# Attention by clusters, then a gated layer: shifts first in a period, a division in another order, an earlier opening

## The chip, the cores and the metric

The kernel runs on one core of a Trainium2 chip. A core has a matrix engine (TensorE, PE in the profile), a vector engine (VectorE, DVE), an engine for curves and copies (ScalarE, ACT), a general one (GpSimd, POOL) and one that here only issues transfers (SyncE, SP). They work beside each other and wait for each other through semaphores; each takes its own instructions in order. SBUF is the memory on the chip and PSUM the small one, in eight banks, that matmuls write. The metric is the device time of one execution in microseconds (us).

## The reference

Two stages. The first is attention in which a query sees only the keys that chose the same one of 16 centroids; the second is a layer with the activation h * erf(softplus(h)).

```python
batch, n_heads, seq, head_dim = (4, 8, 768, 64)
q_assign = np.argmax(np.einsum('bhsd,hcd->bhsc', q_n, c_n), axis=-1)
k_assign = np.argmax(np.einsum('bhsd,hcd->bhsc', k_n, c_n), axis=-1)
mask = q_assign[:, :, :, None] == k_assign[:, :, None, :]
scores = scale * np.matmul(q, k.transpose(0, 1, 3, 2))
scores = np.where(mask, scores, -1000000000.0)
scores = scores - np.max(scores, axis=-1, keepdims=True)
attn = np.exp(scores)
attn = attn / (np.sum(attn, axis=-1, keepdims=True) + 1e-09)
return np.matmul(attn, v).astype(np.float32)
...
h = x @ w_in                      # x: 3072 x 512, w_in: 512 x 2048
sp = np.maximum(h, 0.0) + np.log1p(np.exp(-np.abs(h)))
g = h * erf(sp)
return (g @ w_out).astype(np.float32)
```

`q_n`, `k_n` and `c_n` are q, k and the centroids divided by their lengths.

## The kernel before

**Pairs, halves, units, periods.** Two heads are worked on together as a pair, in the two halves of the 128 partitions; there are 16 pairs. The queries of a pair come in two halves of 384, the keys in six blocks of 128, so a pair has 12 units (`units`), each a block of scores of 128 keys by 2 x 384 queries. `period(p, i)` handles two units; six periods (i = 0 to 5) make a pair, the first three its half 0, the last three its half 1.

**Score and shift.** `products` writes q times k into a bank pair `sc` (two such buffers). `scores` adds, by a second matmul of the 0/1 masks `qm` and `km`, a large negative number where the clusters differ, and for each query a shift, so that the exponential on ACT (`curve`, into one of eight buffers `pr`) needs no maximum of its own. The shift must be known first: `maxima_step` recomputes the masked scores in bf16 with queries on the partitions into the bank pair `wide` (a matmul of `qv` and `kv`, then one of `qm` and `km`), and DVE takes their maximum (`nmx`). A pair needs 12 such steps. After six of them a small reduction makes `lowest`, and `turn` transposes it with three matmuls into a bank `turned[h]`, from which ACT copies one row for each head into `qm`: the row of shifts. `scores` of that half can start only then.

**How far ahead.** A list `ahead` (L689) says which maxima steps belong to which unit: mostly the step seven further on, with one step of pair 1 left out and done by itself at the end of pair 0. `turn` stands before the scores in periods 2 and 5 (L732), one period before the shift is used.

**Sums and division.** `accumulate` adds up the exponentials on POOL, `attend` multiplies them with v into `turned[half]`, both for the units of the period before. When a half is complete (at the end of periods 3 and 0 of the next pair), `divide` sums over partitions with a matmul of -1s (`minus`) into the other `turned` bank and makes 1/sum as exp(-ln(sum)) on ACT (`inv`). In the next period DVE makes one Newton step on it (`den`, two operations) and then the quotient `x`, which reads `turned[half]`; SP stores it in DRAM.

**Choosing.** For the pair after next, `transposes` turns q and k on DVE, `similarities` multiplies by the centroids into `turned[1]`, `choose` finds the winner, and `masks` multiplies by `pick` into a `turned` bank and copies to `qm` or `km` on ACT. `MASKS` (L47) says in which period and at which of four places of it: 0 after the first maxima step, 1 after the products, 2 between the two exponentials, 3 at the end. So the two `turned` banks serve the output, the sums, the similarities, the masks and the shifts in turn.

**Weights.** In spare time, ACT, DVE and POOL convert the layer's weights, which come as 64-bit floats (`size_and_rest`, `bounded`, `sign`, `shifted`, `summed`): two pieces of 512 columns in a pair, 22 pieces in the first 11 pairs. From about 465 us only the layer runs.

**The order.** In the attention all instructions keep the order in which the program writes them on each engine (`InOrder`), so the code above is the schedule. DMAs wait for their slot, for the buffer they write and for the engine that read it last. The opening (L174 to L200, L249 to L279, L794 to L849) loads the centroids and pair 0's q and k from two queues, normalizes the centroids, makes constants, transposes, chooses and does the first seven maxima steps of pair 0.

Of the kernel before, what the change touches and what calls it, by code (L numbers as in the profile page):

```python
# [9 lines left out]
F32 = mybir.dt.float32  # L10
# [9 lines left out]
P = 128  # L20
B, H, S, D = 4, 8, 768, 64
C = 16
# [21 lines left out]
NPT = NJ + 2  # L44
N_LATE = 10
LAST_X = 11
MASKS = {(0, 1): ("k", 0), (0, 2): ("k", 1), (2, 0): ("q", 0), (5, 0): ("q", 1)}  # L47
FIRST_MASKS = {(2, 1): ("k", 0), (2, 3): ("q", 0), (3, 0): ("k", 1), (5, 0): ("q", 1)}


class InOrder:
# [16 lines left out]
def kernel(  # L68
# [65 lines left out]
    def part_of(i, lo, n):  # L134
        return more_out[:, i].rearrange("p f m -> p (f m)")[:, lo : lo + n]
# [14 lines left out]
    def load(p, nm, src, pl):  # L150
        if p >= NPAIR:
            return
        b, h0 = heads(p)
        if nm == "v":
            t = pl.tile([P, NJ, 2, D], F32, name="in_v")
            for e in range(2):
                queues[0].dma_start(out=t[:, :, e], in_=src[b, h0 + e].rearrange("(j p) d -> p j d", p=P))
        else:

            t = pl.tile([P, NB, Q], F32, name="in_" + nm)  # L160
            for e in range(2):
                for g in range(D // Q):
                    queues[e].dma_start(
                        out=t[e * D + g * Q : e * D + (g + 1) * Q],
                        in_=src[b, h0 + e, :, g * Q : (g + 1) * Q].rearrange("(n t) d -> t n d", t=Q),
                    )
        pairs.setdefault(p, {})[nm] = t

    def load_qk(p):
        load(p, "q", q, stage)  # L170
        load(p, "k", k, stage)


    setup = prs[-1].rearrange("p e n -> p (e n)")  # L174
# [2 lines left out]

    load_qk(0)
    queues[1] = sy
    tc.keep_in_program_order(nc.scalar.preload_act_table_set("natural_log_exp_and_others"))  # L180

    make_identity(nc, ident)
# [60 lines left out]
    def summed(n):  # L243
        w, lo = w_steps[n][0].bitcast(I32), steps[n][1].bitcast(I32)
        ge.tensor_tensor(out=w, in0=w, in1=lo, op=ALU.add)
        if n in after_of:
            fetch(after_of[n])

    cn = setup[:, D : 3 * D].rearrange("p (e d) -> p e d", e=2)  # L249
    spare = iter(range(3 * D, HW))  # L250

    def scalar_tile():
        n = next(spare)
        return setup[:, n : n + 1]
# [6 lines left out]
    norm = scalar_tile()  # L261
    ae.activation(out=norm, in_=ss, func=ACT.Ln)
    ae.activation(out=norm, in_=norm, func=ACT.Exp, scale=0.5)
    for it in range(2):
        inv = scalar_tile()
        ve.reciprocal(out=inv, in_=norm)
        twice = scalar_tile()
        ve.scalar_tensor_tensor(
            out=twice, in0=ss, scalar=inv, in1=norm, op0=ALU.mult, op1=ALU.add
        )  # L270
        norm = scalar_tile()
        ve.tensor_scalar(
            out=norm, in0=twice, scalar1=0.5, scalar2=(1e-6 if it else 0.0),
            op0=ALU.mult, op1=ALU.add,
        )
    rden = scalar_tile()
    ve.reciprocal(out=rden, in_=norm)
    for e in range(2):
# [2 lines left out]
    def transposes(p, which="qk"):  # L281

        if p >= NPAIR:
            return
        st = pairs[p]
        for nm in which:
            st[nm + "T"] = rows[p % 3][nm]
            ve.transpose(out=st[nm + "T"], in_=st.pop(nm).rearrange("p n t -> p (n t)"))
        if "k" in which:
            st.update(lows[p % 2])  # L290
            load_qk(p + 1)

    def similarities(p):

# [77 lines left out]
    def turn(p, h):  # L372

        st = pairs[p]
        pn = turned[h][:, 0:HW].rearrange("p (t n) -> p t n", t=HJ)
        for t in range(HJ):
            te.matmul(pn[:, t], lhsT=lowest[h][:, t], rhs=identb, start=True, stop=True)
        for e in range(2):
            r = slice(e * D + SH, e * D + SH + 1)
            ae.copy(  # L380
                out=st["qm"][r, h * HW : (h + 1) * HW], in_=pn[r].rearrange("p t n -> p (t n)")
            )
        st["shift", h] = True
# [34 lines left out]
    def curve(u):  # L418

        pr = prs[u % NPT]  # L420
        ae.activation(out=pr[:, :, 0:HW], in_=sc_of.pop(u)[:, :, 0:HW], func=ACT.Exp, scale=D**-0.5)
# [25 lines left out]
    def divide(u):  # L447

        p, half, _ = units[u]
        st = pairs[p]  # L450
        av = st["av", half]

        psum = turned[1 - half][:, 0:HW]
        for e in range(2):
            te.matmul(
                psum[e * D : (e + 1) * D], lhsT=minus, rhs=st["acc", half][:, e], start=True, stop=True
            )

        if u + 1 < len(units):
            inv = routep.tile([P, HW], F32, name="inv")  # L460
            den = routep.tile([P, HW], F32, name="den")
        else:
            inv, den = part_of(0, 4 * HW, HW), part_of(1, 0, HW)
        ae.activation(out=inv, in_=psum, func=ACT.Ln, bias=alleps, scale=-1.0)
        ae.activation(out=inv, in_=inv, func=ACT.Exp, scale=-1.0)
        yield
        ve.scalar_tensor_tensor(
            out=den, in0=psum, scalar=S * EPS, in1=inv, op0=ALU.subtract, op1=ALU.mult
        )
        ve.scalar_tensor_tensor(  # L470
            out=den, in0=den, scalar=2.0, in1=inv, op0=ALU.add, op1=ALU.mult
        )
        yield
        x = part_of(0, (2 * p + half) % 4 * HW, HW)
        ve.scalar_tensor_tensor(
            out=x, in0=av[:, 0:HW], scalar=av[:, HW : HW + 1], in1=den, op0=ALU.add, op1=ALU.mult
        )
        b, r = divmod(p, HP)
        nc.sync.dma_start(
            out=x_dram[r * P : (r + 1) * P, b * S + half * HW : b * S + (half + 1) * HW], in_=x  # L480
        )
        if half == 1:
            del pairs[p]
        yield
# [201 lines left out]

    ahead = [[] for _ in units]  # L689
    for n in range(NJ + 1, 2 * NJ * NPAIR):  # L690
        if n == 3 * NJ:
            continue
        slot = n - NJ - (n < 2 * NJ or n > 3 * NJ)
        if slot < len(units):
            ahead[slot].append(divmod(n, 2 * NJ))

    def step_ahead(slot):
        for which in ahead[slot]:
            maxima_step(*which)

    forms = sum((left_forms(ve, *w_in_parts(f, 2)) for f in range(0, HF, 2)), [])
    routing = [iter(())]
# [2 lines left out]
    def period(p, i):  # L705
# [7 lines left out]
                return masks(p + 1, *which, turned[0 if i in (0, 5) else 1])  # L713
            return lambda: None

        step_ahead(u)
        mask(0)()
        next(part[0], None)
        products(u)
# [6 lines left out]
        elif (p, i) == (0, 1):  # L726
            similarities(1)
            routing[0] = choose(1)
            next(routing[0], None)
        step_ahead(u + 1)  # L730
        next(part[0], None)
        if i in (2, 5) or (p, i) == (1, 0):  # L732
            for which in turns:
                turn(*which)
            turns.clear()
        scores(u)
        scores(u + 1)
        later = mask(2)
        curve(u)
        later()  # L740
        curve(u + 1)
        if i == 0 and early(n1 - 1):
            shifted(n1 - 1)
        elif i == 1 and early(n1):
            size_and_rest(n1)
        elif i == 2 and early(n1):
            bounded(n1)
            sign(n1)
        elif i == 3:
            if early(n1):  # L750
                shifted(n1)
            if early(n2):
                size_and_rest(n2)
        elif i == 4 and early(n2):
            sign(n2)
        elif i == 5 and early(n2):
            bounded(n2)
        if n1 - (i == 0) >= N_EARLY and i in (0, 2, 3, 5) and forms:
            forms.pop(0)()
        if i == 0:  # L760
            transposes(*((p + 2, "q") if p else (1, "k")))
        elif i == 1:
            load(p + 1, "v", v, vp)
            if p == 0:
                run(routing[0])
                vectors(1, "q")
                vectors(1, "k")
        elif i == 2:
            transposes(p + 2, "k" if p else "qk")
        elif i == 3:  # L770
            next(routing[0], None)
        elif i == 4:
            vectors(p + 2, "k")
        elif i == 5:
            run(routing[0])
            vectors(p + 2, "q")
# [10 lines left out]
                part[0] = divide(u - 1)  # L787
                next(part[0])
        mask(3)()
        if (p, i) == (0, 5):  # L790
            maxima_step(1, NJ)


    pct = turned[0][:, 0:P]  # L794
    te.transpose(out=pct, in_=cn.rearrange("p e d -> p (e d)"), identity=ident)
    ve.memset(nbig, 0.0)
    for e in range(2):
        ve.memset(nbig[e * D : e * D + C], -BIG)
        ve.memset(nbig[e * D + SH : e * D + SH + 1], 1.0)
    for t in maxima:  # L800
        ve.memset(t, FLOOR)
    ve.memset(pick, 0.0)
    ve.tensor_copy(out=identb, in_=ident)
    ve.memset(minus, -1.0)
    ve.memset(alleps, S * EPS)
    for t in lowest:
        ge.memset(t, 0.0)
    st = pairs[0]
    st["qT"], st["kT"] = rows[0]["q"], rows[0]["k"]
    ve.transpose(out=st["qT"], in_=st.pop("q").rearrange("p n t -> p (n t)"))  # L810
# [4 lines left out]
        )  # L815
    ve.transpose(out=st["kT"], in_=st.pop("k").rearrange("p n t -> p (n t)"))
    st.update(lows[0])
    load_qk(1)
    similarities(0)
    vectors(0, "q")  # L820
    vectors(0, "k")
# [6 lines left out]
                )  # L828
    also = ps_s.tile([P, 2, 512], F32, name="sc", tag="s")
    products(0)  # L830
    run(choose(0))
    transposes(1, "q")
    copies = [
        masks(0, nm, half, bank)
        for nm, half, bank in (("q", 0, wide[:, 0]), ("k", 0, turned[0]), ("k", 1, turned[1]))
# [2 lines left out]
    for copy in copies[1:]:  # L838
        copy()
    load(0, "v", v, vp)  # L840
    for n in range(PLACES):
        fetch(n)
    queues[0] = queues[1] = nc.sync
    for i in range(NJ):
        maxima_step(0, i, also if i % 2 else wide)
    turn(0, 0)
    turns.clear()
    masks(0, "q", 1, turned[1])()
    maxima_step(0, NJ)  # L849
    for p in range(NPAIR):  # L850
        for i in range(HJ * 2):
            period(p, i)
# [115 lines left out]
```

## Time and profile before

| | us |
|---|---|
| median of 3 runs | 1052.33 |
| lowest, highest | 1051.50, 1052.68 |
| the profiled execution | 1051.62 |
| its span, first to last instruction | 1049.9 |

| stretch of the profile | what runs | us |
|---|---|---|
| 0 to 28.4 | opening, up to the first exponential of scores | 28.4 |
| 28.4 to 63.9 | pair 0 and period 0 of pair 1 | 35.5 |
| 63.9 to 352.4 | pairs 1 to 11 with weight conversion | 288.5 |
| 352.4 to 465 | the other pairs | 112.6 |
| 465 to 1049.9 | the layer | 585 |

Where each half of a pair ends there is a group of four `turned<-more_out,minus` matmuls (the sum over partitions). Their distance gives the pitch: 13.93 and 13.60 us for the two halves of a pair in mid-run.

In the lines of the timeline the columns are the start, the duration, the engine, the line, the operation, what it writes and reads, the shapes, the number merged, and in brackets the engine's idle time before it with what ended it. Most lines carry L59, that of the helper which records every operation; the tile names tell which it is. In the table of stretches the columns are the stretch and its length, the busy us of PE, PEld (weight loads), DVE, ACT and POOL with the number of instructions, the granted PE clock, the share of the DMA engines and their GB/s.

### The profile page before, as it was taken

The page shows a single profiled execution, that of the slowest core. Times are in us where ns is not written, and L with a number is a line of the kernel's source. Part 1 is how long each engine was busy: PE and PEld are TensorE (multiplying, and loading weights), DVE is VectorE, ACT ScalarE, POOL GpSimd, SP SyncE. Part 2 cuts the span into 40 slices and gives each one's busy share as a digit, 9 for nine tenths or more (in the row PEclk, how much of TensorE's full clock was granted, in tenths as well). Part 3 has the DMA queues.
Part 4 walks back from the last instruction along what each step waited for, and adds up shares of the span by engine and source line. Part 5 has one row for each costly group of instructions (what it writes and reads, how often), then busy time and mean ns, then how long its engine had stood idle before and what let it go on. Part 6 is the DMA issues. An engine that isn't in the chain of part 4 may idle for free.

```text
span 1049.9 us, 15192 instructions
## 1 busy us (share of the span) xinstructions
PE 1023.1 (97%) x5793; PEld 708.3 (67%) x5793; DVE 706.8 (67%) x1307; ACT 514.5 (49%) x674; POOL 337.7 (32%) x229
## 2 busy tenths in 40 slices
PE   4899999999999999999999999999999999999998
PEld 1344444444444444448888888888888888888887
DVE  6667777777777777747976656476465656564754
ACT  2667777777777666547643250505143222415050
POOL 1566777777667666666230000000000000000000
PEclk8999999999999999999999999999999999999999
DMA  8344443433342321113200010001011000000001
GB/s 191 61 101 101 97 97 94 100 94 88 86 101 51 94 57 31 31 67 117 81 0 19 23 41 1 21 22 39 1 41 41 1 11 31 1 1 21 21 1 40
DMA packets 141496, 55.53 MB, mean 53 GB/s; under 512 B 127088, under 2 KB 131184, under 8 KB 141424
## 3 DMA queue, kind: packets, MB, share of 16 engines
q1 hardware_dynamic: 138288, 54.18, 20.1%
q8 instruction: 45, 0.74, 0.3%
q10 hardware_dynamic: 3136, 0.39, 0.2%
q14 instruction: 27, 0.22, 0.1%
HBM read 41.98 MB, written 12.58 MB: 52 GB/s over the span
## 4 chain that ended last, share of the span: by engine, by line
PE 90%; DVE 6%; ACT 2%; issue 1%; POOL 1%; ACTq 0%; DVEq 0%; POOLq 0%
PE bank L59 42%; PE turned L59 29%; PE sc L59 13%; PE wide L59 7%; DVE nmx L59 3%; DVE den L59 2%; ACT pr L59 1%; POOL more_out L59 1%; ACT inv L59 1%; ACT qm L59 0%; ACT x_own L59 0%; ACT w_in L59 0%; ACTq L59 0%; DVE pr L59 0%; ACT L180 0%
## 5 line engine op out<-in xcount | busy, mean ns | idle before, releaser
L59 POOL TENSOR_TENSOR more_out<-more_out,pr 128x768 f32<-128x768 f32 x128 | 215.8, 1686 | 99.7 <-ACT pr L59 94.6
L59 DVE TENSOR_REDUCE nmx<-wide 128x2 f32<-128x768 f32 x189 | 180.3, 954 | 84.9 <-PE wide L59 83.0
L59 ACT ACTIVATE pr<-sc 128x768 f32<-128x768 f32 x192 | 146.9, 810 | 67.2 <-PE sc L59 66.4
L59 PE MATMUL turned<-pr,in_v 128*64 128x386 f32 x768 | 145.4, 500 | 0.1
L59 DVE TENSOR_TENSOR g<-bank,g 128x256 f32<-128x256 f32 x222 | 89.5, 421 | 56.7 <-PE bank L59 46.4
L59 PE MATMUL bank<-x_own,w_in 128*128 128x256 f32 x424 | 104.4, 379 | 0.0
L59 PE MATMUL bank<-w_out,g 128*128 128x256 f32 x448 | 103.1, 379 | 0.0
L59 PE MATMUL sc<-qT,kT 64*128 64x384 f32 x528 | 101.3, 494 | 0.0
L59 PEld LDWEIGHTS bank<-w_out,g 128*128 128x128 f32 x448 | 85.1, 190 | 11.6
L59 PEld LDWEIGHTS turned<-pr,in_v 128*64 128x64 f32 x768 | 46.6, 136 | 67.8 <-issue 63.2
L59 PEld LDWEIGHTS bank<-x_own,w_in 128*128 128x128 f32 x424 | 80.4, 190 | 12.1 <-issue 1.2
L59 PEld LDWEIGHTS <-qv 64*128 64x128 bf16 x384 | 27.2, 94 | 87.8 <-issue 75.2
L59 ACT COPY g<-bank 128x256 f32<-128x256 f32 x28 | 10.4, 372 | 152.1 <-PE bank L59 148.5
L59 DVE TENSOR_TENSOR osb<-bank,osb 128x256 f32<-128x256 f32 x87 | 35.4, 420 | 72.9 <-ACT osb L59 25.4
L59 ACT ACT_TABLE_LOAD x48 | 61.6, 1283 | 45.7 <-DVE g L59 45.1
L59 POOL TENSOR_TENSOR more_out<-pr,pr 128x768 f32<-128x768 f32 x32 | 58.4, 1826 | 62.6 <-ACT pr L59 62.6
L59 PE MATMUL bank<-x_more,more_in 128*128 128x256 f32 x296 | 76.0, 379 | 0.0
L59 PE MATMUL wide<-kv,qv 64*128 64x384 bf16 x378 | 68.6, 333 | 6.3 <-DVE nmx L59 4.0
L59 PE MATMUL wide<-km,qm 64*128 64x384 bf16 x378 | 67.2, 329 | 2.7 <-ACT qm L59 2.7
L59 PEld LDWEIGHTS sc<-qT,kT 64*128 64x128 f32 x528 | 52.2, 189 | 25.0 <-ACT pr L59 6.0
L59 PE MATMUL bank<-more_out,g_more 128*128 128x256 f32 x272 | 64.3, 379 | 0.0
L59 DVE TENSOR_TENSOR g<-a_s,g 128x512 f32<-128x512 f32 x96 | 62.5, 688 | 1.4 <-ACT a_s L59 1.4
(153 smaller groups left out, 1688.3 us busy)
## 6 DMA issues: line engine op xcount, KB each, us to landing
x_own<-in_moe_w_in_dram SPq DMA_DIRECT2D x13, 512.0 KB, 4.1
in_v<-in_v_dram SPq DMA_DIRECT2D x32, 192.0 KB, 2.9
x_dram<-more_out SPq DMA_DIRECT2D x32, 192.0 KB, 2.5
x_own<-x_dram SPq DMA_DIRECT2D x6, 1024.0 KB, 5.2
out_dram<-osb SPq DMA_DIRECT2D x24, 256.0 KB, 2.0
in_q<-in_q_dram SPq DMA_DIRECT2D x62, 96.0 KB, 3.0
in_k<-in_k_dram SPq DMA_DIRECT2D x62, 96.0 KB, 2.6
g_more<-in_moe_w_out_dram SPq DMA_DIRECT2D x6, 512.0 KB, 3.5
```

Source lines behind the costliest of these rows:

```text
L59: ins = getattr(self.engine, name)(*args, **kw)
```

## The change

- `turn` moves to the first place of periods 0 and 3, the periods that use the shift. The list `ahead` goes: unit u does the maxima step six further on, with unit 0 and 1 of pair 0 handled by themselves. The masks of q move from place 0 to place 1 of periods 2 and 5.
- `divide` makes one part of the Newton step (`den`), multiplies the output by the raw `inv`, and in the second place multiplies by the correction.
- The opening: the centroids' length has one Newton step in place of two; the constants are written before it; pair 1's q and k are loaded right behind pair 0's, into `x_more`, and pair 2's follow; pair 1's q is transposed before pair 0's choice, its k after the seventh maxima step; the mask of q's second half is made after the second; the weights' piece that goes to `x_more` is loaded after pair 1's k has been read.

```diff
-MASKS = {(0, 1): ("k", 0), (0, 2): ("k", 1), (2, 0): ("q", 0), (5, 0): ("q", 1)}
-FIRST_MASKS = {(2, 1): ("k", 0), (2, 3): ("q", 0), (3, 0): ("k", 1), (5, 0): ("q", 1)}
+MASKS = {(0, 1): ("k", 0), (0, 2): ("k", 1), (2, 1): ("q", 0), (5, 1): ("q", 1)}
+FIRST_MASKS = {(2, 1): ("k", 0), (2, 3): ("q", 0), (3, 0): ("k", 1), (5, 1): ("q", 1)}
...
-            t = pl.tile([P, NB, Q], F32, name="in_" + nm)
+            if pl is None:
+                t = x_more.rearrange("p a k t -> p (a k t)")[:, (nm == "k") * S : (1 + (nm == "k")) * S]
+                t = t.rearrange("p (n t) -> p n t", t=Q)
+            else:
+                t = pl.tile([P, NB, Q], F32, name="in_" + nm)
...
     load_qk(0)
     queues[1] = sy
+    load_qk(1)
...
+    ve.memset(nbig, 0.0)
...
+    for t in lowest:
+        ge.memset(t, 0.0)
...
-    for it in range(2):
-        inv = scalar_tile()
-        ve.reciprocal(out=inv, in_=norm)
...
+    inv = scalar_tile()
+    ve.reciprocal(out=inv, in_=norm)
...
-        ve.scalar_tensor_tensor(
-            out=den, in0=den, scalar=2.0, in1=inv, op0=ALU.add, op1=ALU.mult
-        )
-        yield
         x = part_of(0, (2 * p + half) % 4 * HW, HW)
         ve.scalar_tensor_tensor(
-            out=x, in0=av[:, 0:HW], scalar=av[:, HW : HW + 1], in1=den, op0=ALU.add, op1=ALU.mult
-        )
+            out=x, in0=av[:, 0:HW], scalar=av[:, HW : HW + 1], in1=inv, op0=ALU.add, op1=ALU.mult
+        )
+        yield
+        ve.scalar_tensor_tensor(out=x, in0=den, scalar=2.0, in1=x, op0=ALU.add, op1=ALU.mult)
...
-    ahead = [[] for _ in units]
-    for n in range(NJ + 1, 2 * NJ * NPAIR):
-        if n == 3 * NJ:
-            continue
-        slot = n - NJ - (n < 2 * NJ or n > 3 * NJ)
-        if slot < len(units):
-            ahead[slot].append(divmod(n, 2 * NJ))
-
-    def step_ahead(slot):
-        for which in ahead[slot]:
-            maxima_step(*which)
+    def step_ahead(u):
+        p, i = divmod(u + NJ, 2 * NJ)
+        if p < NPAIR:
+            maxima_step(p, i)
...
-        step_ahead(u)
+        if u > 0:
+            for which in turns if i in (0, 3) else ():
+                turn(*which)
+                turns.remove(which)
+            step_ahead(u)
...
-        step_ahead(u + 1)
+        if u > 0:
+            step_ahead(u + 1)
         next(part[0], None)
-        if i in (2, 5) or (p, i) == (1, 0):
-            for which in turns:
-                turn(*which)
-            turns.clear()
...
+        if u == 0:
+            step_ahead(1)
...
-        if (p, i) == (0, 5):
-            maxima_step(1, NJ)
...
-    load_qk(1)
+    load_qk(2)
...
     products(0)
+    transposes(1, "q")
     run(choose(0))
-    transposes(1, "q")
...
-    for n in range(PLACES):
+    for n in range(PLACES - 1):
         fetch(n)
-    queues[0] = queues[1] = nc.sync
     for i in range(NJ):
         maxima_step(0, i, also if i % 2 else wide)
+        if i == 1:
+            masks(0, "q", 1, turned[1])()
+    step_ahead(0)
     turn(0, 0)
     turns.clear()
-    masks(0, "q", 1, turned[1])()
-    maxima_step(0, NJ)
+    transposes(1, "k")
+    fetch(PLACES - 1)
+    queues[0] = queues[1] = nc.sync
```

More of the change, by code (lines that the diff above doesn't have):

```diff
@@ L169, in load_qk @@
     def load_qk(p):
-        load(p, "q", q, stage)
-        load(p, "k", k, stage)
+        load(p, "q", q, stage if p != 1 else None)
+        load(p, "k", k, stage if p != 1 else None)
     setup = prs[-1].rearrange("p e n -> p (e n)")
@@ L247, in summed @@
             fetch(after_of[n])
+    ve.memset(nbig, 0.0)
+    for e in range(2):
+        ve.memset(nbig[e * D : e * D + C], -BIG)
+        ve.memset(nbig[e * D + SH : e * D + SH + 1], 1.0)
+    for t in maxima:
+        ve.memset(t, FLOOR)
+    ve.memset(pick, 0.0)
+    ve.tensor_copy(out=identb, in_=ident)
+    ve.memset(minus, -1.0)
+    ve.memset(alleps, S * EPS)
+    for t in lowest:
+        ge.memset(t, 0.0)
     cn = setup[:, D : 3 * D].rearrange("p (e d) -> p e d", e=2)
@@ L263 @@
     ae.activation(out=norm, in_=norm, func=ACT.Exp, scale=0.5)
-    for it in range(2):
-        inv = scalar_tile()
-        ve.reciprocal(out=inv, in_=norm)
-        twice = scalar_tile()
-        ve.scalar_tensor_tensor(
-            out=twice, in0=ss, scalar=inv, in1=norm, op0=ALU.mult, op1=ALU.add
-        )
[L271 to L274, printed above, removed]
-        )
+    inv = scalar_tile()
+    ve.reciprocal(out=inv, in_=norm)
+    twice = scalar_tile()
+    ve.scalar_tensor_tensor(out=twice, in0=ss, scalar=inv, in1=norm, op0=ALU.mult, op1=ALU.add)
+    norm = scalar_tile()
+    ve.tensor_scalar(out=norm, in0=twice, scalar1=0.5, scalar2=1e-6, op0=ALU.mult, op1=ALU.add)
     rden = scalar_tile()
@@ L290, in transposes @@
             st.update(lows[p % 2])
-            load_qk(p + 1)
+            if p > 1:
+                load_qk(p + 1)
     def similarities(p):
@@ L469, in divide @@
         )
+        x = part_of(0, (2 * p + half) % 4 * HW, HW)
         ve.scalar_tensor_tensor(
-            out=den, in0=den, scalar=2.0, in1=inv, op0=ALU.add, op1=ALU.mult
+            out=x, in0=av[:, 0:HW], scalar=av[:, HW : HW + 1], in1=inv, op0=ALU.add, op1=ALU.mult
         )
         yield
-        x = part_of(0, (2 * p + half) % 4 * HW, HW)
-        ve.scalar_tensor_tensor(
-            out=x, in0=av[:, 0:HW], scalar=av[:, HW : HW + 1], in1=den, op0=ALU.add, op1=ALU.mult
-        )
+        ve.scalar_tensor_tensor(out=x, in0=den, scalar=2.0, in1=x, op0=ALU.add, op1=ALU.mult)
         b, r = divmod(p, HP)
@@ L760, in period @@
         if i == 0:
-            transposes(*((p + 2, "q") if p else (1, "k")))
+            if p:
+                transposes(p + 2, "q")
         elif i == 1:
@@ L789, in period @@
         mask(3)()
-        if (p, i) == (0, 5):
-            maxima_step(1, NJ)
     pct = turned[0][:, 0:P]
     te.transpose(out=pct, in_=cn.rearrange("p e d -> p (e d)"), identity=ident)
[L796 to L807, printed above, removed]
     st = pairs[0]
```

## The prediction

> **What bounds the kernel now.** I read four views in this order: the page's table of engines, busy time by stretch, the timeline of the opening, and the timelines of TensorE (PE), VectorE (DVE) and ScalarE (ACT) over one pair of heads in mid-run.
>
> ```profile
> PE 1023.1 (97%) x5793; PEld 708.3 (67%) x5793; DVE 706.8 (67%) x1307; ACT 514.5 (49%) x674; POOL 337.7 (32%) x229
> ...
> 15.70:28.40 12.70, 8.50 (x45) 3.16 (x41) 7.91 (x10) 1.45 (x4) 0.00 (x0) 0.53 0.83 244
> 28.40:63.87 35.47, 29.55 (x207) 12.85 (x205) 24.12 (x34) 23.85 (x36) 18.89 (x12) 0.97 0.33 66
> 63.87:352.40 288.53, 285.77 (x2038) 127.33 (x2038) 220.50 (x314) 216.47 (x331) 205.22 (x126) 1.00 0.42 96
> 465.00:1050.00 585.00, 581.52 (x2694) 510.75 (x2692) 361.31 (x795) 200.78 (x192) 35.79 (x29) 1.00 0.08 28
> ```
>
> PE sets the time from 64 us on. The stretch from 465 us (the dense layers) is solid and the change leaves it alone. What can move is the opening, where PE is idle for some 20 of 64 us and its clock stands at half for a while, and whatever hides inside the "busy" 288 us.
>
> ```profile
> 5.38 0.16 DVE L59 RECIPROCAL pr<-pr 128x1 f32<-128x1 f32 x1
> 6.58 0.48 DVE L59 MEMSET nbig<- 128x1 f32 x5
> 7.46 0.97 DVE L59 STREAM_TRANSPOSE qT<-in_q 128x768 f32<-128x768 f32 x1
> 13.68 0.94 DVE L59 STREAM_TRANSPOSE qT<-in_q 128x768 f32<-128x768 f32 x1
> 21.43 0.18 DVE L59 TENSOR_REDUCE lowest<-nmx 128x6 bf16<-128x18 f32 x1
> 24.27 0.96 DVE L59 TENSOR_REDUCE nmx<-wide 128x2 f32<-128x768 f32 x1 [2.66 <-PE wide L59]
> 28.38 1.51 ACT L59 ACTIVATE pr<-sc 128x768 f32<-128x768 f32 x2 [4.71 <-PE sc L59]
> ```
>
> DVE carries the opening: a chain of tiny operations, constants, transposes, six reductions, then a pause of 2.66 us. The first exponential comes only at 28.38.
>
> ```profile
> 203.56 1.11 DVE L59 SCALAR_TENSOR_TENSOR den<-den,inv 128x384 f32<-128x384 f32 x1
> 204.59 0.95 DVE L59 TENSOR_REDUCE nmx<-wide 128x2 f32<-128x768 f32 x1
> 205.46 0.61 DVE L59 SCALAR_TENSOR_TENSOR more_out<-turned,den 128x384 f32<-128x384 f32 x1
> 205.59 0.34 PE L59 MATMUL wide<-kv,qv 64*128 64x384 bf16 x2
> 205.75 0.34 PE L59 MATMUL wide<-km,qm 64*128 64x384 bf16 x2
> 206.12 0.32 PE L59 MATMUL turned<-hotT,pick 64*128 64x384 bf16 x1
> 221.15 0.50 ACT L59 ACTIVATE qm<-turned 128x384 bf16<-128x384 f32 x1
> 221.70 0.34 PE L59 MATMUL wide<-km,qm 64*128 64x384 bf16 x2
> ```
>
> Here the page's 99% hides stalls. The reduction ends at 205.54 and PE's next step starts at 205.59, although its previous matmuls ended at 205.45. The mask matmul comes 0.37 after the km step (0.16 is usual), just after the quotient has read its bank (205.46 + 0.61). In the other half the km step comes at 221.70, as the mask's copy on ACT (221.15 + 0.50) ends.
>
> **What the Trainium skill says.** "SBUF — State Buffer", section "Who interferes with whom": a DVE instruction with two SBUF inputs contends with a GpSimd instruction that reads SBUF. The trace agrees in kind: the second `den` operation (both inputs in SBUF) takes 0.56 to 1.11 us, mean 0.954 from 60 to 350 us, while the quotient, of the same size with one input in PSUM, takes a steady 0.606. "TensorE: Matmul & The Clock Gate", Part 1: the array runs at half clock until it has been busy for some 3.4 us. The trace agrees: granted 0.50 from 17 to 30 us, 0.94 from 30 to 32. The same page, under "Architectural detail", calls ACT and DVE strict FIFO, which is why a copy on ACT has to be costed with all that stands before it. "DMA: Bandwidth & Descriptors", "Issuing engines are not separate DMA queues": loads from SP and ACT share the 16 engines, so pair 1's loads, issued earlier, queue with pair 0's.
>
> **The change, part by part: the opening.** One Newton step goes: three operations from 5.38 to 6.02, 0.64 us. The constants (6.58 to 7.46, 0.88) move into DVE's wait for the centroids before 2.84. So the q transpose starts near 6.0 in place of 7.46. Pair 0's q was issued by 1.75 and lands at most 3.3 later, 5.1; k was in by about 6.1 (the DMA share falls from 1.28 to 0.07 there) and is needed at 7.4. Eight loads of pair 1 move ahead on SP's queue, from 8.46 to about 3.7. At the 0.8 MB in 4 us that pair 0 took, its q is in near 8.3, needed at 9.0, its k near 10.5, needed at 21. Pair 2's eight loads now stand ahead of v and the weights; at 0.52 us an issue SP reaches the weights at about the old 14.1, because it no longer sits idle from 3.6 to 8.5. I cost that at nothing; each us of late q would cost one us.
>
> The q transpose of pair 1 (0.94) leaves the place between `hotT` and `qm` and goes beside the similarity matmuls, where DVE waits 0.92. `hotT` comes 1.36 earlier and `qm` does not wait: the first reduction moves from 15.75 to about 14.0, the sixth's end from 21.32 to 19.6. The mask of q's second half is now made among the six, so the seventh reduction follows without the pause of 2.66. `turn` follows at 19.9: 0.5 of matmuls, 0.95 of copies, while PE makes 1.28 of products. Scores start near 21.8, the first exponential at 22.4: 6.0 earlier. But two maxima steps that used to be done by then now come after, and with one `wide` buffer and half clock a step and its reduction take 0.84 + 0.97. Carried on with the durations of before, the scores of units 2 and 3 come at 28.7 (32.47), the end of period 3 at 44.3 (47.57; there `turn` waits for a copy behind ACT's 1.36 us sign operation, as long as the old 1.88 stall), the end of period 5 at 52.0 (57.35), since a reduction's 1.28 and 1.05 waits go, and pair 1's period 1 starts at 57.3 (63.87). I take 6.5 us, with 4 to 8 as bounds.
>
> **The steady pairs.** A pair is 27.54 us (13.93 + 13.60) from pair 1 to 10, and 26.67 (13.53 + 13.14) in pairs 11 to 13, which have no weight conversion beside them: 0.87 of each early pair is waiting. With the old order, period 1 has nmx, den, den, nmx, quotient on DVE; now nmx, den, quotient, nmx, correction. The second nmx starts at 1.42 + 0.58 + 0.65 = 2.65 after the period's start, against 3.03, and ends at 3.6; PE arrives at 0.33 + 1.29 + 0.33 + 0.42 + 1.45 = 3.82. That wait (0.21 and 0.11 in a pair) goes. The quotient has then freed its bank before the masks, which also stand after the products: 2 x 0.21 and 2 x 0.10 go. The mask of q's second half is used a period later: 0.19 and 0.11 go. `turn` between a step and the scores costs 0.25 before and 0.28 after it in the clean pair (385.45 to 386.14 less 0.16); at a period's start, behind full-height matmuls, I take 0.33, so 0.2 goes twice. That makes about 1.2, or 26.35 a pair.
>
> What is late next? The correction has two SBUF inputs, so about 0.95, and begins at 3.6 beside the accumulations on POOL; it can hold the next nmx by 0 to 0.2, in two periods. I take 0.2 a pair. `turn`'s copies (0.95) stand on ACT behind the previous period's work. In period 3: the mask's copy to 2.46, exponentials to 3.87, sign (next starts 1.09 later) to 4.96, copies to 5.9; the similarities want that bank at 3.82 + 0.33 + 0.33 + 1.38 = 5.86: a wait of 0.1, bounds 0 to 0.4. In period 0: exponentials, cast to 4.67, copies to 5.65; the mask wants the bank at 5.8: none, bounds 0 to 0.3. Queued behind on PE are the step, the scores and all after, so any lateness is paid in full. Net 0.9 a pair, bounds 0.3 to 1.2: 10 pairs, 9 us. Pairs 11 to 14 have no such waits and gain about 0.35 each from `turn` alone: 1.3.
>
> **Sum.** 6.5 + 9 + 1.3 = 16.8. The profiled execution took 1051.62 (span 1049.9 and 1.7 around it), 0.7 below the median of 1052.33: 1034.8, or 1035.5 on the median's footing.
>
> **Rivals.** (1) The steady gain is half given back: the correction meets POOL and `turn`'s copies come late by 0.25 at both places, 0.7 a pair, 7 us: 1042.5. For it: ACT is busy 75% there and my slack is 0.1. Against: ACT waits for PE before most exponentials (33 us of idle). Chance 0.2. (2) Slower: at the first instructions of periods 0 and 3, PE waits for `turn`'s copies behind ACT's queue, twice in each of 15 pairs. It decides from 16.8 / 30 = 0.56 us beyond my figures each; at 0.75 it is +22.5 - 16.8: 1058. Nothing in the trace puts ACT that late unless the 1.36 us sign and a cast both slip behind. Chance 0.06. (3) The clearing does nothing: the early loads hold up pair 0's k and the stalls come back in another place, 1052 within 2. Chance 0.03. (4) The half clock ends early because the opening is denser, and no new wait appears: 8 + 12 + 1.5, 1031 or less. Chance 0.1. My forecast has 0.61.
>
> **The numbers.** 1035.5. The range goes from 1029 to 1047, which takes in both bounds of the pair's cost and rival 1 and leaves out the slower cases and the extreme of rival 4. Faster 0.91, the same 0.03, slower 0.06; within 0.2%, 2.1 us, a measurement of this kernel tells nothing.
>
> **What would show it.** First q transpose near 6.0; first nmx near 14.0; first exponential on scores near 22.4; pair 1's period 1 near 57; distance of the `minus` matmuls two halves apart near 26.6 in mid-run in place of 27.54; the correction 0.9 us long; PE's matmuls after `turn` without a wait on ACT. I am wrong if PE waits on `turned` at the similarities or at the k mask by more than 0.5, if the transpose of pair 1's q waits for its load, or if the pair's pitch stays above 27.2.

## The result, and the profile after

| | before | after |
|---|---|---|
| median (us) | 1051.75 (6 runs) | 1060.74 (6 runs) |
| lowest, highest | 1051.28, 1052.68 | 1059.26, 1060.98 |
| span of the profiled execution | 1049.9 | 1058.9 |
| ratio, 95% interval | | 1.008, 1.0067 to 1.0093 |

The change made the kernel slower by 0.8%; 1035.5 had been forecast. The page of the kernel after, its table of engines and its chain of work (the chain before had PE at 90% and DVE at 6%):

```profile
PE 1018.8 (96%) x5793; PEld 703.1 (66%) x5793; DVE 725.1 (68%) x1304; ACT 517.4 (49%) x674; POOL 357.1 (34%) x229
...
PE 76%; DVE 13%; ACT 7%; issue 2%; POOL 1%; ACTq 0%; DVEq 0%; POOLq 0%
```

DVE has three instructions fewer and is busy 18.3 us longer; POOL has the same 229 and is busy 19.4 us longer. Nothing was added that could take so long, so some instructions must be standing. The opening is not where it happens. DVE and ACT in the timeline of the opening after:

```profile
5.92 0.97 DVE L59 STREAM_TRANSPOSE qT<-in_q 128x768 f32<-128x768 f32 x1
8.95 0.98 DVE L59 STREAM_TRANSPOSE qT<-x_more 128x768 f32<-128x768 f32 x1
13.98 0.96 DVE L59 TENSOR_REDUCE nmx<-wide 128x2 f32<-128x768 f32 x1 [0.69 <-PE wide L59]
22.38 1.51 ACT L59 ACTIVATE pr<-sc 128x768 f32<-128x768 f32 x2 [0.97 <-PE sc L59]
```

Each of these is where the forecast had put it (6.0, 9.0, 14.0, 22.4), and pair 1's q is there without a wait. Pair 1's period 1 starts at 58.87 in place of 63.87: 5.0 us are won. Then they are lost. The halves of a pair, measured between groups of `minus` matmuls, were 13.93 and 13.60 us (27.53 a pair) and are 13.78 and 14.87 (28.65): 1.12 us more in each of ten pairs, and 13.42 and 14.38 in pairs 11 to 13 against 13.53 and 13.14. The layer's first `bank` matmul comes at 474.08 in place of 465.10, 9.0 us late, and from there to the end both take 584.8 us.

The groups of DVE with shapes apart, after, from 60 to 350 us (busy, mean ns of one, idle before):

```profile
L59 DVE SCALAR_TENSOR_TENSOR more_out<-den,more_out 128x384 f32<-128x384 f32 x21 | 25.6, 1218 | 0.0
L59 DVE TENSOR_TENSOR hot<-sims,mx 128x384 bf16<-128x384 f32 x10 | 20.4, 2039 | 0.0
```

The first is the correction of the division; the second, which the change doesn't touch, marks each row's winning cluster. Before, the same view had it at a quarter:

```profile
L59 DVE TENSOR_TENSOR hot<-sims,mx 128x384 bf16<-128x384 f32 x10 | 5.5, 551 | 0.0
```

One such place in the timeline after (pair 6, periods 4 and 5; DVE, POOL, ACT and PE, in order of time):

```profile
219.26 3.63 POOL L59 TENSOR_TENSOR more_out<-more_out,pr 128x768 f32<-128x768 f32 x2 [0.74 <-ACT pr L59]
219.40 1.96 DVE L59 SCALAR_TENSOR_TENSOR more_out<-den,more_out 128x384 f32<-128x384 f32 x1
221.28 0.94 DVE L59 TENSOR_REDUCE nmx<-wide 128x2 f32<-128x768 f32 x1
222.28 0.34 PE L59 MATMUL wide<-kv,qv 64*128 64x384 bf16 x2 [0.59 <-DVE nmx L59]
222.82 0.96 DVE L59 TENSOR_REDUCE nmx<-wide 128x2 f32<-128x768 f32 x1 [0.59 <-PE wide L59]
223.04 1.51 ACT L59 ACTIVATE pr<-sc 128x768 f32<-128x768 f32 x2 [0.82 <-PE sc L59]
223.82 0.18 DVE L59 TENSOR_REDUCE lowest<-nmx 128x6 bf16<-128x18 f32 x1
224.00 3.81 POOL L59 TENSOR_TENSOR more_out<-more_out,pr 128x768 f32<-128x768 f32 x2 [1.10 <-ACT pr L59]
224.24 2.04 DVE L59 TENSOR_TENSOR hot<-sims,mx 128x384 bf16<-128x384 f32 x1
226.31 0.58 DVE L59 STREAM_TRANSPOSE hotT<-hot 128x384 bf16<-128x384 bf16 x1
226.81 0.92 DVE L59 TENSOR_REDUCE nmx<-wide 128x2 f32<-128x768 f32 x1
226.95 0.33 PE L59 MATMUL turned<-hotT,pick 64*128 64x384 bf16 x1 [0.39 <-DVE hotT L59]
227.79 0.34 PE L59 MATMUL wide<-kv,qv 64*128 64x384 bf16 x2 [0.51 <-DVE nmx L59]
```

Both long instructions begin 0.14 and 0.24 us after an accumulation on POOL. The lines merge two accumulations; in narrower windows the first of each stands alone:

```profile
219.26 1.68 POOL L59 TENSOR_TENSOR more_out<-more_out,pr 128x768 f32<-128x768 f32 x1 [0.74 <-ACT pr L59]
224.00 1.86 POOL L59 TENSOR_TENSOR more_out<-more_out,pr 128x768 f32<-128x768 f32 x1 [1.10 <-ACT pr L59]
```

They end at 220.94 and 225.86. The correction ends 0.42 us after the one, `hot` 0.42 after the other, and each takes 0.55 where nothing meets it. So they are not slowed all along; they stand for the rest of POOL's instruction, and the profile books that as busy time. The order of the two decides. In the other half of the pair the correction begins 0.05 us before POOL:

```profile
234.08 0.55 DVE L59 SCALAR_TENSOR_TENSOR more_out<-den,more_out 128x384 f32<-128x384 f32 x1
234.13 2.04 POOL L59 TENSOR_TENSOR more_out<-more_out,pr 128x768 f32<-128x768 f32 x1 [0.47 <-ACT pr L59]
```

There it takes 0.55, and the accumulation takes 2.04 in place of 1.68. Of the 21 corrections from 60 to 350 us, 11 are of this kind and 10 stand for 1.93 to 1.97 us. In the half with `hot`, PE waits three times, 0.59 for the reduction behind the correction, 0.39 for `hotT`, 0.51 for the reduction behind it. The kernel before at the corresponding place:

```profile
222.08 0.96 DVE L59 TENSOR_REDUCE nmx<-wide 128x2 f32<-128x768 f32 x1 [0.94 <-PE wide L59]
222.35 0.95 ACT L59 CAST qm<-turned 1x384 bf16<-1x384 f32 x2 [0.70 <-PE turned L59]
223.29 0.55 DVE L59 TENSOR_TENSOR hot<-sims,mx 128x384 bf16<-128x384 f32 x1
223.32 1.51 ACT L59 ACTIVATE pr<-sc 128x768 f32<-128x768 f32 x2
224.28 3.43 POOL L59 TENSOR_TENSOR more_out<-more_out,pr 128x768 f32<-128x768 f32 x2 [2.02 <-ACT pr L59]
```

Here the two copies of `turn` stood on ACT before the exponentials, and POOL, which waits for the first exponential, started 0.99 us after `hot` had started, and 0.44 after it had ended. POOL follows the start of the exponentials by 0.96 us in both kernels. But `hot` starts 0.03 before that start in the one and 1.20 after it in the other, a shift of 1.23. Counted from the maximum before `hot` (222.08 and 222.82), the exponentials start 1.02 earlier, as `turn`'s matmuls and copies no longer stand between, and `hot` starts 0.21 later, as the small reduction to `lowest` now does. The length of the correction has no part in it: in run 6 below, where it takes 0.54, `hot` still starts 0.24 after POOL.

PE's waits from 66 to 450 us (in total, times, longest), after, and the same view before:

```profile
PE wide L59 <- DVE nmx L59: 12.5, 23, 0.6
PE turned L59 <- DVE hotT L59: 6.0, 13, 0.7
PE turned L59 <- ACT qm L59: 2.9, 10, 0.3
```

```profile
PE wide L59 <- DVE nmx L59: 0.6, 4, 0.2
```

### The profile page after: what moved, and what is told of

Same layout as the page of the kernel before. It is cut to its first block, busy times and chain, and to the rows that moved or that the text cites. A ratio compares the mean times of both kernels' runs of the same rounds, so it can differ in the third digit from the quotient of the medians.

```text
span 1058.9 us, 15207 instructions
## 1 busy us (share of the span) xinstructions
PE 1018.8 (96%) x5793; PEld 703.1 (66%) x5793; DVE 725.1 (68%) x1304; ACT 517.4 (49%) x674; POOL 357.1 (34%) x229
## 4 chain that ended last, share of the span: by engine, by line
PE 76%; DVE 13%; ACT 7%; issue 2%; POOL 1%; ACTq 0%; DVEq 0%; POOLq 0%
PE bank L59 41%; PE turned L59 23%; PE sc L59 7%; DVE nmx L59 5%; PE wide L59 5%; DVE hot L59 3%; DVE more_out L59 2%; ACT pr L59 2%; ACT x_own L59 2%; ACT qm L59 1%; ACT inv L59 1%; DVE hotT L59 1%; POOL more_out L59 1%; DVE den L59 1%; ACT w_in L59 0%
## 5 line engine op out<-in xcount | busy, mean ns | idle before, releaser
L59 POOL TENSOR_TENSOR more_out<-more_out,pr 128x768 f32<-128x768 f32 x128 | 235.3, 1838 | 57.3 <-ACT pr L59 52.2
L59 PE MATMUL sc<-qT,kT 64*128 64x384 f32 x528 | 99.1, 494 | 0.0
L59 PEld LDWEIGHTS sc<-qT,kT 64*128 64x128 f32 x528 | 49.3, 191 | 25.0 <-issue 2.6
```

The source lines that it names most:

```text
L59: ins = getattr(self.engine, name)(*args, **kw)
```

## Experiments

**Theory A.** While POOL reads SBUF, a DVE operation with both inputs there stands until POOL's instruction is over. The move of `turn` brings an accumulation just ahead of `hot`, the new division gives the correction two SBUF inputs beside another, and both hold the maximum behind them, for which PE waits. **Rival B.** `turn`'s copies on ACT come late (the prediction's slower rival), or the division's or the opening's new timing makes the loss, with the long `hot` a sign of it.

Eleven kernels ran. Ratios are to the kernel before on the same chip (medians 1052.1 to 1052.3); halves are those of mid-run, the one of periods 4, 5 and 0 first.

| kernel | us | ratio, 95% interval | halves (us) | `hot`, correction (mean us) |
|---|---|---|---|---|
| after, old division | 1057.77 | 1.0052, 1.0037 to 1.0067 | 14.20, 14.16 | 2.04, none |
| after, `hot` in period 3 | 1053.31 | 1.0010, 1.0003 to 1.0017 | 14.15, 13.79 | 0.56, 0.55 |
| both of these | 1055.77 | 1.0032, 1.0019 to 1.0045 | 14.15, 13.99 | 0.56, none |
| after, no sums in period 0 | 1044.99 | 0.9931, 0.9912 to 0.9951 | 13.80, 13.78 | 0.55, 1.18 |
| after, `mx` in PSUM | 1048.12 | 0.9950, 0.9933 to 0.9967 | 13.87, 13.78 | 0.55, 1.22 |
| after, product in PSUM | 1052.48 | 0.9998, 0.9990 to 1.0007 | 14.11, 13.78 | 2.04, 0.54 |
| after, both in PSUM | 1038.84 | 0.9870, 0.9855 to 0.9885 | 13.12, 13.79 | 0.55, 0.54 |
| before, new division | 1051.59 | 0.9994, 0.9985 to 1.0002 | 13.90, 13.53 | 0.55, 1.22 |
| after, `turn` put back | 1047.68 | 0.9954, 0.9938 to 0.9971 | 13.91, 13.53 | 0.55, 1.22 |
| that, both in PSUM | 1043.77 | 0.9922, 0.9905 to 0.9938 | 13.60, 13.53 | 0.55, 0.54 |
| both in PSUM, step first | 1035.87 | 0.9846, 0.9831 to 0.9861 | 13.12, 13.46 | 0.55, 0.54 |

In the same order the kernel before has 13.60 and 13.93, the kernel after 14.87 and 13.78.

**1. The old division in the kernel after.**

```diff
-            out=x, in0=av[:, 0:HW], scalar=av[:, HW : HW + 1], in1=inv, op0=ALU.add, op1=ALU.mult
+            out=den, in0=den, scalar=2.0, in1=inv, op0=ALU.add, op1=ALU.mult
...
-        ve.scalar_tensor_tensor(out=x, in0=den, scalar=2.0, in1=x, op0=ALU.add, op1=ALU.mult)
+            out=x, in0=av[:, 0:HW], scalar=av[:, HW : HW + 1], in1=den, op0=ALU.add, op1=ALU.mult
```

> The changed kernel with the division of before (correction first, on DVE ahead of the second maximum; the product last). Theory A (DVE and POOL shut each other out: an operation of DVE with two SBUF inputs stands still while an accumulation runs, and the change brings the accumulations to where such operations stand): the correction no longer meets the accumulation at the start of period 5, so the half pitch of 14.87 falls by 0.9 to about 14.0, the other may grow by 0.2, and the time falls by 7 to 9, to about 1052. Rival B (the row of shifts comes late through ACT's queue, and the long operations on DVE only fill a wait that PE has anyway): no change, 1060.

It won 3 us where 7 to 9 were expected, and `hot` stayed at 2.04. The half with `hot` fell by 0.67, the other grew by 0.38, as the old `den` operation, which also has two SBUF inputs, stands too (mean 1.04). As both orders of the division meet POOL, this run doesn't tell what the meeting costs; run 6 does.

**2 and 3. `hot` made earlier, with the new and the old division.**

```diff
+        if i == 3:
+            next(routing[0], None)
+            next(routing[0], None)
         if i == 0 and early(n1 - 1):
             shifted(n1 - 1)
...
-        elif i == 3:
-            next(routing[0], None)
```

> The changed kernel with the comparison that makes hot (two SBUF inputs) moved from period 5 to period 3, right behind the maximum it needs, where POOL is idle; all else as it is. Theory A: hot takes 0.55 again in place of 2.04, the waits of PE for hotT and for the maximum behind it go (1.39 a pair), the half pitch of 14.87 falls to about 13.5 and the time by some 20, to about 1041. Rival B: the k mask has to wait for ACT's copies of the shifts in the same bank, so 1058 to 1060.

> Both edits in the changed kernel: the division of before, and hot in period 3. Theory A: the two gains add, half pitches near 13.8 and 13.0, time 1032 to 1036. Rival B: 1058 to 1060.

`hot` fell to 0.56, and 7 us came back where 20 were expected: the next operation on DVE took its place. In run 3 the two gains were to add up, and it is 2.5 us slower than run 2; its old `den` operation takes 0.84 us in the mean, where run 2's correction takes 0.55. The timeline of run 2, DVE and POOL:

```profile
212.16 0.56 DVE L59 TENSOR_TENSOR hot<-sims,mx 128x384 bf16<-128x384 f32 x1
212.39 2.03 POOL L59 TENSOR_TENSOR more_out<-pr,pr 128x768 f32<-128x768 f32 x1 [2.35 <-ACT pr L59]
212.63 2.07 DVE L59 TENSOR_SCALAR w_in<-w_in 128x512 uint32<-128x512 uint32 x1
214.62 0.95 DVE L59 TENSOR_REDUCE nmx<-wide 128x2 f32<-128x768 f32 x1
```

`hot` began first and is not touched; it is POOL that takes 2.03 in place of 1.82. `shifted` (0.41 alone) follows, has one input, and stands for the rest of POOL's instruction. Moving `hot` handed the block on to the next operation. In pairs 11 to 13, where `shifted` doesn't run, a sum over weights with two SBUF inputs was next (2.31 to 2.33 us, others of its kind 0.68), and the half stayed at 14.40.

**4. The other party taken away: POOL's two accumulations of period 0 are left out** (those that run beside `hot`; the sum of half 1 then lacks two of its six blocks of keys).

```diff
-                accumulate(w)
+                if i > 0:
+                    accumulate(w)
```

> The changed kernel without the two accumulations that POOL makes in period 0: the exponentials of the last two key blocks of each pair's second half are left out of the sum. Nothing else is moved, so hot stands where it stood. Theory A: hot takes 0.55, the half pitch with period 0 falls from 14.87 to about 13.5, the correction stays above 1.1 in mid-run, time about 1041. Rival B: hot may be short, but the pitch stays above 14.5 and the time above 1056.

The timeline of run 4, DVE, with `hot` in its old place:

```profile
214.30 2.01 DVE L59 SCALAR_TENSOR_TENSOR more_out<-den,more_out 128x384 f32<-128x384 f32 x1
219.19 0.55 DVE L59 TENSOR_TENSOR hot<-sims,mx 128x384 bf16<-128x384 f32 x1
```

`hot` takes 0.55, the half falls from 14.87 to 13.80 (expected: 13.5, and 1041 us in all), and the time is below that of before, although every copy of `turn` stands on ACT as in the kernel after. Rival B's ACT falls with it: `turn`'s copies cost PE the 0.29 us a pair seen at the similarities, and its list shows no other wait for them. The correction, whose POOL neighbour is still there, stands at 2.01.

**5, 6 and 7. One operand in PSUM, nothing moved.** `mx` goes into unused columns of `wide`; the raw product goes back to the bank it was read from; then both.

```diff
-        mx = routep.tile([P, n], F32, name="mx")
+        mx = wide[:, 1, 512 - n : 512]
```

```diff
-            out=x, in0=av[:, 0:HW], scalar=av[:, HW : HW + 1], in1=inv, op0=ALU.add, op1=ALU.mult
+            out=av[:, 0:HW], in0=av[:, 0:HW], scalar=av[:, HW : HW + 1], in1=inv, op0=ALU.add, op1=ALU.mult
...
-        ve.scalar_tensor_tensor(out=x, in0=den, scalar=2.0, in1=x, op0=ALU.add, op1=ALU.mult)
+        x = part_of(0, (2 * p + half) % 4 * HW, HW)
+        ve.scalar_tensor_tensor(out=x, in0=den, scalar=2.0, in1=av[:, 0:HW], op0=ALU.add, op1=ALU.mult)
```

> mx is written into spare PSUM columns of `wide`, so that `hot` reads one operand from SBUF and one from PSUM; nothing is moved. Theory A (hot stands because it and POOL's accumulation both read two SBUF operands): hot falls from 2.04 to 0.55-0.65 us where it stands, the half of periods 3-5 from 14.87 to 13.6-13.9 us, pairs 11-13 from 14.38 to about 13.1; the correction stays at up to 2 us; time 1043-1046 us. Rival (hot is late for its inputs, or any VectorE operation beside GpSimd is slow): hot stays near 2 us, time 1058-1061 us.

> The raw product is written back to its PSUM bank, so that the correction reads one operand from PSUM and den from SBUF; hot is left as it is. Theory A: the correction is 0.55-0.65 us everywhere (after: mean 1.22, up to 2), the half of 14.87 falls to about 14.0, the other stays near 13.8, hot stays at 2.04; time 1051-1055 us. Rival (the correction's length hides nothing on the path, since hot alone holds the tensor engine): 1058-1061 us.

> Both of the two edits before. Theory A: no operation of VectorE with two SBUF operands is left beside the accumulations of periods 1-5; halves of 13.8 and 13.0-13.2 us in pairs 1-10, 13.4 and 13.1 in pairs 11-13; time 1032-1040 us, under the kernel before. Rival (GpSimd's port then blocks another operation, as it did `shifted`): one half stays above 14 us, time 1045-1055 us.

The timeline of run 5, POOL and DVE, at the place of the collision:

```profile
219.66 3.62 POOL L59 TENSOR_TENSOR more_out<-more_out,pr 128x768 f32<-128x768 f32 x2 [1.10 <-ACT pr L59]
219.90 0.55 DVE L59 TENSOR_TENSOR hot<-sims,wide 128x384 bf16<-128x384 f32 x1
```

The order is the same as in the kernel after, POOL 0.24 us ahead, and `hot` runs through beside it in 0.55 us. This is the cleanest test of the set: same place, same work, one operand elsewhere. A pair fell by 1.00 us with `mx` in PSUM (28.65 to 27.65), by 0.76 with the product (27.89), by 1.74 with both (26.91): the two blocks are separate and add up. Run 5 came out 2 us above its band of 1043 to 1046: the half of 13.87 is as expected, but pairs 11 to 13 have one of 13.39 and not of 13.1. Run 7 is 13.4 us faster than before. What PE waits for in it, from 66 to 450 us:

```profile
PE turned L59 <- ACT qm L59: 3.0, 10, 0.3
PE wide L59 <- DVE hot L59: 0.8, 3, 0.3
PE turned L59 <- POOL more_out L59: 0.2, 1, 0.2
```

The second line is new and is the price of the edit: `hot` now reads a column of `wide`, so in pairs 11 to 13 the next maxima step waits 0.28 us for it, and the half is 13.39 there in run 7 too.

**8. The new division alone, in the kernel before** (the edit of run 1 the other way).

> The kernel before with the new order of the division alone (periods 2 and 5 turn in step 1 as before, old prologue). Theory A: POOL's accumulations start where they did, so hot stays at 0.55 us; the correction lengthens to 1-2 us where it meets POOL, and holds the maxima behind it: -3 to +6 us, 1049-1058. Rival (the division's order alone makes the loss): hot at 2 us or a half above 14.5, 1060-1066 us.

No change that can be told: the half of periods 1 to 3 gained 0.40, the other lost 0.30, with the correction standing at up to 1.96 us beside POOL. `hot` is at 0.55: the long correction alone doesn't bring POOL ahead of it.

**9 and 10. The kernel after with `turn` put back** (the hunks of the change at `MASKS`, `ahead`, `step_ahead` and the `turns` loop undone), without and with the two PSUM operands.

```diff
-        if u > 0:
-            for which in turns if i in (0, 3) else ():
-                turn(*which)
-                turns.remove(which)
-            step_ahead(u)
+        step_ahead(u)
...
+        if i in (2, 5) or (p, i) == (1, 0):
+            for which in turns:
+                turn(*which)
+            turns.clear()
```

> The changed kernel with `turn`, the maxima steps' slots and q's masks put back to where they were; the new opening and the new division stay. Theory A (the move of `turn` lets POOL start ahead of `hot`): hot back to 0.55 us, pitches 13.53 and 13.90 us as with the division alone, the opening's 5 us kept; time 1045-1048 us, so that the move of `turn` by itself costs the changed kernel some 13 us. Rival (the opening's shift in time, not `turn`, brings POOL onto hot): hot stays at 2 us, a half above 14.5, 1056-1061 us.

> The kernel with both operands in PSUM (1038.8 us), and `turn` put back as in the run before. It tells what the move of `turn` brings once the blocking is out. If my steps for the pairs were right but for the blocking, `turn`'s place is worth 0.2-0.4 us a pair: a pair of 27.1-27.3 us here against 26.90, time 1041-1045 us. Rival (the move brings nothing even then): 26.9 us or less a pair, 1036-1039 us.

The timeline of run 9, DVE and POOL: `hot` is through before POOL starts again, as in the kernel before.

```profile
219.92 0.55 DVE L59 TENSOR_TENSOR hot<-sims,mx 128x384 bf16<-128x384 f32 x1
220.92 3.44 POOL L59 TENSOR_TENSOR more_out<-more_out,pr 128x768 f32<-128x768 f32 x2 [2.13 <-ACT pr L59]
```

The place of `turn`, with the maxima steps' slots and q's masks that moved with it, costs the kernel after 1060.7 - 1047.7 = 13 us. With both operands in PSUM the same move gains: 1043.8 against 1038.8, 27.13 against 26.91 us a pair. The opening is in both and doesn't bring POOL onto `hot`; against the division alone it gains some 4 us (1051.6 - 1047.7).

**11. The last wait.** In run 7's kernel, the second maxima step of period 3 is written before the similarities.

```diff
         if i == 3:
+            step_ahead(u + 1)
             similarities(p + 2)
...
-        if u > 0:
+        if u > 0 and i != 3:
             step_ahead(u + 1)
```

> The kernel with both operands in PSUM, and in period 3 the maxima step of the second unit made before the similarities, so that the step (0.33 us) stands in the wait of 0.30 us for `turn`'s copies. If that wait is all that is left in a pair: 26.6 us a pair in place of 26.90, time 1035-1037 us. Rival (the step then waits for its own buffer or for the maximum before it): 26.9 us or more, 1038-1041 us.

The waits for `qm` are gone from PE's list, and the half falls from 13.79 to 13.46 us. What remains from 66 to 450 us are the other two lines of run 7's list, with the same numbers. This is the fastest of the set: 1.5% faster than before, 24.9 us faster than the changed one (1060.74 - 1035.87).

## Why the prediction was wrong

**The opening was right.** Its marks came within 0.1 us, which is partly luck: in the runs with the same opening and `turn` in its new place, the first exponential starts at 22.37 to 23.29. Pair 1's period 1 came at 58.87 for 57.3. The half before it took 14.87 us and takes 13.11 in run 7, without the blocks; with that it would have come at 57.1. So the 6.5 us were there, and 1.8 of them were lost to the two blocks. The half clock ran differently from what was read: the prediction took the trace to agree that it ends after some 3.4 us of work, but from 16.7 to 20 us of the kernel before PE was busy for 2.97 of 3.3 us, and it was granted 0.50 until about 30 all the same. What ends it stays open here; from 20 to 25 us the kernel after was granted 0.50, and run 7, with the same opening, 1.00.

**The gross gain of a pair was over-sized, but real.** 1.2 was forecast. The terms listed for it add up to 1.64 (0.32, 0.62 and 0.30 of waits, 0.4 for `turn`), and their waits of 1.24 are more than the 0.87 by which an early pair is longer than one without weight conversion; the 1.2 is near 0.87 + 0.35, and how it was reached isn't said. Run 11, where neither a block nor a wait for `qm` is left in these pairs, has 27.53 - 26.58 = 0.95. The similarities' wait for `turn`'s copies was priced at 0.1 with bounds of 0 to 0.4, and measures 0.29.

**The step that failed is "What is late next?".** It priced the correction at about 0.95, the mean of the old `den` operation, holding the next maximum by 0 to 0.2 us, together 0.2 a pair. It measures up to 1.97, and costs 0.76 a pair (run 6). And it asked only about the operation that the change adds. It followed `turn`'s copies to where they go on ACT and not to what their leaving sets free: the exponentials of period 5 start earlier against DVE's work, POOL's accumulation with them, and `hot` was only 0.99 us ahead of POOL, against a shift of 1.23. That costs 1.00 a pair (run 5), and is wholly missing from the sum. Together 1.76 in place of 0.2: it turns the -0.9 into -0.9 + 1.56 = +0.66, and the over-sized gross gain (0.25) and the wait (0.2) make +1.1; 1.12 was measured. Pairs 11 to 13 were to gain 0.35 each and lost 1.13, by `hot` alone.

**What was read too shortly.** The prediction named the place in the Trainium skill that bears on this ("SBUF — State Buffer", section "Who interferes with whom"), and took it as a slowing. The section goes further, in its item on performance modes: "Whoever issues first gets the shared pair for the whole instruction", and the other blocks. The trace agrees, for two SBUF inputs as well: `hot` 2.04 us behind POOL, and 0.56 when it comes first. The mean of 0.954 was no price for the correction. From 60 to 350 us not one of the 21 old `den` operations was free: they took 0.77 to 1.13, each behind a shorter instruction of POOL, a sum over weights of 1.3 us, and each ended 0.41 to 0.42 after it. The 0.56 that the prediction gives as the lower end comes from after 350 us, where no weights are converted. POOL and DVE of the kernel before:

```profile
202.97 1.28 POOL L59 TENSOR_TENSOR w_in<-w_in,x_own 128x512 int32<-128x512 int32 x1
203.56 1.11 DVE L59 SCALAR_TENSOR_TENSOR den<-den,inv 128x384 f32<-128x384 f32 x1
381.83 0.56 DVE L59 SCALAR_TENSOR_TENSOR den<-den,inv 128x384 f32<-128x384 f32 x1
```

With the same 0.42 behind an accumulation of 1.68 us, an estimate for the correction is up to 2.1. The trace of before even showed a standing `hot`, in pair 0 (POOL, DVE and PE of its timeline):

```profile
33.80 3.63 POOL L59 TENSOR_TENSOR more_out<-more_out,pr 128x768 f32<-128x768 f32 x2 [2.00 <-ACT pr L59]
34.26 1.63 DVE L59 TENSOR_TENSOR hot<-sims,mx 128x384 bf16<-128x384 f32 x1
36.56 0.32 PE L59 MATMUL turned<-hotT,pick 64*128 64x384 bf16 x1 [0.43 <-DVE hotT L59]
```

With that line, and a lead of 0.99 us from which `turn`'s copies alone take 0.95, the forecast could have had, as a rival, a block of up to an accumulation (1.68 us) in every pair.

**The rivals.** The first (half given back) had the correction meet POOL, at 0.7 a pair together with late copies. The slower one named 1058, near the result, for waits of 0.75 us at two places of a pair for `turn`'s copies; PE has one of 0.29, so the nearness is luck. The signs set for being wrong did their work: the pair's pitch is above 27.2, while PE's wait at the similarities stayed under 0.5.

**What stays open.** That it is the leaving of `turn`'s matmuls and copies, and the new place of the small reduction, which brings POOL ahead of `hot` is read from the traces. Runs 9 and 10 show only that it is the place of `turn` together with the maxima steps' slots and q's masks; none of these was moved by itself.

## What to carry to other kernels

Before moving work, list VectorE's operations with two SBUF inputs (here an integer shift with one belonged to them too) and the GpSimd instructions nearest to each, with the time between their starts: that lead is what a shift can use up, and the price beyond it is up to a whole GpSimd instruction plus whatever queues behind. Where the mean of an operation lies well above that of a like one, some of its cases are standing, so price it place by place. If one operand can lie in PSUM, the collision can go away without moving anything, whereas moving the operation may hand it to the next.

## What the runs showed of the hardware

- A VectorE operation with two SBUF inputs that starts behind a GpSimd one stands until that is over, and the profile shows it as busy: 0.55 became 2.04 us for `hot`, 1.93 to 1.97 for the standing corrections and 0.77 to 1.13 for the old `den`. Each of these 41, from 60 to 350 us, ended 0.41 to 0.42 us after GpSimd's instruction. With one operand in PSUM `hot` took 0.55 at the same place.
- An integer shift with one SBUF input was held as well: 0.41 became 2.07 us behind a 2.03 us GpSimd instruction. In the kernel before, 7 of its 15 from 60 to 350 us already took 0.68 to 0.69, behind accumulations. The Trainium skill's same section lists tensor_scalar among the operations that can take the shared ports in a two-port mode; that fits, but no run tests the mode by itself.
- GpSimd pays too: an accumulation that starts 0.05 us behind a correction took 2.04 us in place of 1.68. In the mean, those onto a running sum took 1.68 us from 60 to 350 us before, and 1.82 after.
- PSUM as a place for an intermediate made the operations no slower: the product written there took 0.62 us against 0.61, the correction reading it 0.54 against 0.55 when free. For `mx` there was a price beside: PE's wait of 0.28 us for the bank in pairs 11 to 13.
